# Turning a third of the softmax tiles with VectorE and transfers instead of TensorE, and other first transfers, in a fused attention and gated feed-forward kernel

## The chip, the core and the metric

One of the eight cores of a Trainium2 chip. The metric is device time of one execution in microseconds (us). Before the change: 924.59 us, median of three runs from 923.99 to 927.79.

## What is computed

Attention whose weights below the row's maximum less tau are set to zero, then a feed-forward network with a convolution of three taps over the tokens and a gate. Sizes: 8 batches, 8 heads, 576 tokens, 64 columns per head; 512 model columns, 1024 inner columns.

```python
scores = scale * np.matmul(q, k.transpose(0, 1, 3, 2))
thresh = np.max(scores, axis=-1, keepdims=True) - tau
scores = np.where(scores >= thresh, scores, -1000000000.0)
attn = np.exp(scores - np.max(scores, axis=-1, keepdims=True))
attn = attn / (np.sum(attn, axis=-1, keepdims=True) + 1e-09)
attn_out = np.matmul(attn, v)
...
h = np.maximum(x @ w_in, 0.0)
for k in range(K):
    conv_out += conv_w[k][None, None, :] * hp[:, k:k + S, :]
gate = 1.0 / (1.0 + np.exp(-conv_out))
return (h * gate @ w_out).astype(np.float32)
```

## The kernel before, in words

Two heads form a pair; a batch has four pairs. The 576 tokens of a batch are five tiles, four of 128 and one of 64, in two chunks: tiles 0 and 1, then tiles 2, 3 and 4. A *unit* is one tile of one pair; 20 units make a batch, 160 the kernel.

**A unit** (`unit`, from L516). TensorE writes the scores of each head to PSUM (`ps_s`, L537 in batch 0 and for the small tile, L544 elsewhere). VectorE takes the row maximum (`top`, L552), one of three engines makes the threshold (`limit`, L556 or L558), ScalarE the exponential (`exp`, L561), and VectorE sets what lies below the threshold to zero and sums the row (`mask`, L564). A small chain forms the inverse of the sum (L581 to L588), and `norm` (L595 on ScalarE, L597 elsewhere) scales the tile `em`, 128 rows by 2 x 576 columns.

**Transposes** (from L608). The product with v needs `em` turned. TensorE turns it in nine blocks of 128 x 128 (L626), in two groups of four into a bank of PSUM (`ps_t`), and the ninth blocks of a pair's tiles together in a last group. ScalarE evicts each group to `eT` (L621), 512 columns at a time, or the ninth blocks side by side. `attend` (L676, L685) multiplies `eT` by v for two pairs at once; ScalarE and VectorE split the result into a high and a low part, `x` (L692, L695).

**Feed-forward.** `mm1` (L713) multiplies `x` by the first weights; `relu` (L728), three taps (`tap0` L732 or L734, then L748), tanh (L757) and the gate (L755) follow, and a split into `gh` and `gl`. `mm2` (L786) multiplies by the second weights; ScalarE evicts 128 tokens to `ot` (L793) and SP's queue writes them out (L794).

**Loads.** SP's queue issues the loads of k (L451, L487), q (L452, L502), v (L513) and of the weights (L363), and copies inside SBUF, `halves` (L477), that bring heads from one half of the partitions to the other for `ks`, `q1` and `q2`. At the start, ScalarE's queue issues the loads of the first pair's k and of the first three pieces of weights.

**The order.** Nothing runs where it is written. Each operation goes to a `Plan` (L83) with its engine, a cost in ns, what it reads and writes, and a due time: the number of its unit less a lead from the table `AHEAD`. `Plan.run` plays all engines forward and takes, on each, the ready operation with the earliest due time; it keeps buffers and costs of its own. An operation with several possible engines can leave its first one when that has more than `BACKLOG` ns of work; `NORM`, `TAP` and `LOW` name the first engine of normalizations, first taps and low parts; `KEEP` and `SWITCH` order TensorE's kinds of matmul; `MOE` says how `mm1` and `mm2` alternate. What comes out is a fixed list of instructions for each engine. Four `em`, two `eT`, two `q1`, two `q2` and two `v` buffers exist.

Of the kernel before, what the change touches and what calls it, by code (L numbers as in the profile page):

```python
# [20 lines left out]
AHEAD = {'s': 6.25, 's4': 7.75, 't': 3.5, 'a': 3.5, 'prep': 4.25, 'w': 2.5, 'load': 7.75}  # L21
# [13 lines left out]
BACKLOG = {'pool': 6860.0, 'dve': 120.0, 'act': 9000000000.0}  # L35
WRATE = (1.225, 1.745)
ALT = 11.76
# [4 lines left out]
EARLY = 1  # L42
# [6 lines left out]

JOINT = 2  # L50

KEEP = {'rows': 2.304, 'cols': 1.613, 'turn': 3.226, 'full': 2.304}
# [30 lines left out]
class Plan:  # L83
# [32 lines left out]
    def run(self):  # L116
# [35 lines left out]
        while events:  # L152
# [25 lines left out]
            for e in ready:  # L178
# [4 lines left out]
                while ready[e]:  # L183
# [6 lines left out]
                    if e == home or load[home] + max(free[home] - t, 0.0) > BACKLOG[home]:  # L190
# [55 lines left out]
def tile_tau_attention_gated_ffn(  # L246
# [14 lines left out]
    nc = tc.nc  # L261
# [32 lines left out]

    def const(name, shape, dtype):
        return plan.buf(cpool, name, 1, shape, dtype, name)
# [30 lines left out]
    def sp(n):  # L327
        return 2.6 * n
# [13 lines left out]
    def split(src, n, name, high, low, hr, lr, queue="sp"):  # L342
# [17 lines left out]
        w = AHEAD["w"]  # L360

        def load():
            (nc.sync if queue == "sp" else nc.scalar).dma_start(flat().bitcast(I64), src)  # L363
# [16 lines left out]
        if queue == "sp":  # L380
            op("sp", sp(2 * n), load, w=[hi, lo], ahead=w + AHEAD["load"])
        else:
            op("act", 450, load, w=[hi, lo], ahead=90, late=sp(2 * n) + LATENCY["sp"])
# [37 lines left out]
    def load_weight(i):  # L421
        if i < W1N:
            src, dst, c, f = w_in, w1, i % NCB, i // NCB
        else:
# [4 lines left out]
            src[c * P:(c + 1) * P, f], WN, f"stage_{i}", h, l, *((x, (c, f.start)) for x in dst), "act" if i < 3 else "sp"  # L429
# [14 lines left out]
    def prep_rows(i, b, p, o, w, tag):  # L444
# [3 lines left out]
        a = AHEAD["prep"]  # L448

        if i:  # L450
            op("sp", sp(S + D), lambda: nc.sync.dma_start(k[:], kp[b, p]), w=[(k, 0), (k, 1)], ahead=a + 2)  # L451
            op("sp", sp(2 * w), lambda: nc.sync.dma_start(q[:], qd[b, p, :, :, o:o + w]), w=[(q, 0), (q, 1)], ahead=a + 2)  # L452
        else:
            for j, on in enumerate((slice(0, CH), slice(CH, S + D))):
                op(
                    "act", 450, lambda on=on: nc.scalar.dma_start(k[:, on], kp[b, p, :, on]), w=[(k, j)], ahead=210 - 10 * j,
                    late=1500 + sp(CH) * (1 + j)
                )
                op(
                    "sp", sp(w) + 400, lambda j=j: nc.sync.dma_start(q[:, j], qd[b, p, :, j, o:o + w]), w=[(q, j)], ahead=210 - 10 * j  # L460
                )
# [21 lines left out]
    def prep_k(b, p, ks):  # L483

        a = AHEAD["prep"]
# [11 lines left out]
    def prep_q(i, b, p, q1, q2):  # L497
# [3 lines left out]
        a = AHEAD["prep"]  # L501
# [9 lines left out]
    def load_v(i, b, p):  # L511
        vt = plan.buf(wk, "v", 2, [P, NBLK, D], F32, f"v_{i}")
        op("sp", sp(NBLK * D), lambda: nc.sync.dma_start(vt[:], vc[b, p]), w=[(vt, 0)], ahead=AHEAD["prep"])  # L513
        return vt

    def unit(u, k, q1, q2, o, n):  # L516
# [8 lines left out]
        a = AHEAD["s" if 2 * n > P else "s4"]  # L525
# [81 lines left out]

    def transposes(u, ems, tiles, eT):  # L608


        em, n, off = ems[-1]

        def group(i, reads, parts, *evacs, width=4 * P):
# [3 lines left out]
                "pe", width * 0.852, lambda: parts(pt), w=[(pt, 0)], r=reads + [(ident, 0)], ahead=AHEAD["t"], kind="turn"  # L617
            )
            for k, (w, dst, src) in enumerate(evacs):
                op(  # L620
                    "act", act(w, True), lambda dst=dst, src=src: nc.scalar.activation(dst(), src(pt), AF.Copy),  # L621
                    w=[(eT, (off, i, k))], r=[(pt, 0)], ahead=AHEAD["t"]
# [15 lines left out]
        if n < P:  # L638
# [9 lines left out]
        full, small = ([x for x in ems if (x[1] < P) == y] for y in (False, True))  # L648
# [3 lines left out]
        def odd(pt):  # L652
            for x in full + small:
                turn(pt, x[2], x[0], 8 if x[1] == P else 3.5)

        parts = [(w, lambda: eT[:, 8, :w], lambda pt: pt[:, :w])]
        for _, m, at in small:
            for j in range(2):
                parts.append((
                    m, lambda j=j: eT[j * D:(j + 1) * D, 4, at:at + m], lambda pt, j=j: pt[D:, w + j * m:w + (j + 1) * m]  # L660
# [3 lines left out]
    def attend(of, w, parts):  # L664

        pas = [plan.buf(ps_t, "ps_t", 2, [P, 512], F32, f"pa_{i}") for i, *_ in of]
        a = AHEAD["a"]
# [287 lines left out]
```

## Time and profile before

| | before |
|---|---|
| median of three runs | 924.59 us |
| the profiled execution | 925.54 us |
| its span, first to last instruction | 923.8 us |
| granted clock of TensorE | 0.996 |
| packets of the transfers | 77,926, of them 18,560 under 512 bytes |
| bytes moved | 104.02 MB |
| HBM read and written | 58.88 and 9.44 MB |

PE is TensorE's matmul, PEld its weight load, DVE VectorE, ACT ScalarE, POOL GpSimd; SP's and ACT's queues issue transfers (SPq, ACTq). A group's row reads: line, engine, operation, what is written and read, shape, count, then busy us and mean ns of one, then the idle time just before and what ended it. A timeline's row: start and length in us, engine, line, operation and count.

### The profile page before, as it was taken

How to read it: one execution, taken by the hardware profiler on the slowest of the kernel's cores; microseconds unless marked ns; L12 is line 12 of the kernel's file. 1: busy time of each engine (PE TensorE's matmuls, PEld its weight loads, DVE VectorE, ACT ScalarE, POOL GpSimd, SP SyncE). 2: the span in 40 equal slices, each digit the busy share in tenths (PEclk: the TensorE clock that was granted, in tenths of full speed). 3: DMA queues.
4: the chain of work that ended last, by engine and by line, in shares of the span. 5: the costliest groups of instructions: out<-in, count | busy, mean ns of one | idle time of the engine just before them, and what ended most of it. 6: DMA issues, size and time to landing. Idle time of an engine off the chain costs nothing.

```text
span 923.8 us, 19667 instructions
## 1 busy us (share of the span) xinstructions
PE 896.7 (97%) x6308; PEld 731.8 (79%) x6308; DVE 741.1 (80%) x1853; ACT 701.2 (76%) x1590; POOL 582.1 (63%) x1028
## 2 busy tenths in 40 slices
PE   5989899999999999999999999999999999999998
PEld 2446588878889788879888787887888888887897
DVE  5988999979868798878967789886977879896643
ACT  5888898878678787869768687786958788785653
POOL 3665887767747586666746677675865757664422
PEclk9999999999999999999999999999999999999999
DMA  6643363355341652345423453416523265221000
GB/s 211 200 151 128 97 166 101 111 146 167 87 122 40 176 150 83 84 115 140 122 91 81 133 148 103 120 59 166 161 85 95 55 175 140 83 79 60 13 24 34
DMA packets 77926, 104.02 MB, mean 113 GB/s; under 512 B 18560, under 2 KB 49536, under 8 KB 77824
## 3 DMA queue, kind: packets, MB, share of 16 engines
q1 hardware_dynamic: 76960, 100.86, 38.6%
q10 hardware_dynamic: 864, 1.90, 0.6%
q8 instruction: 51, 0.84, 0.4%
q14 instruction: 51, 0.42, 0.1%
HBM read 58.88 MB, written 9.44 MB: 74 GB/s over the span
## 4 chain that ended last, share of the span: by engine, by line
PE 79%; ACT 9%; DVE 6%; issue 2%; DMA 2%; POOL 1%; SPq 0%; ACTq 0%; POOLq 0%; DVEq 0%
PE po L786 21%; PE ph L713 16%; PE ps_t L626 13%; PE pa L685 12%; PE ps_s L544 11%; PE ps_s L537 4%; ACT eT L621 2%; PE pa L676 2%; DVE em L564 2%; ACT em L561 2%; DVE few L552 1%; DVE t L748 1%; PE pw_stage L394 1%; DMA q<-in_qd_dram 1%; ACT hp L728 1%
## 5 line engine op out<-in xcount | busy, mean ns | idle before, releaser
L597 POOL TENSOR_SCALAR em<-em,few 128x576 f32<-128x576 f32 x285 | 258.3, 914 | 36.9 <-DVE few L588 27.3
L564 DVE SCALAR_TENSOR_TENSOR em<-ps_s,few,em 128x576 f32<-128x576 f32 x288 | 228.1, 812 | 51.0 <-ACT em L561 44.9
L713 PE MATMUL ph<-x,w1h 128*128 128x322 f32 (+1 forms) x1024 | 243.2, 305 | 0.7 <-ACT hp L728 0.7
L552 DVE TENSOR_REDUCE few<-ps_s 128x1 f32<-128x576 f32 x288 | 210.8, 748 | 29.4 <-PE ps_s L537 15.2
L561 ACT ACTIVATE em<-ps_s,few 128x576 f32<-128x576 f32 x288 | 206.7, 743 | 30.9 <-DVE few L552 26.0
L621 ACT ACTIVATE eT<-ps_t 128x512 f32<-128x512 f32 (+2 forms) x416 | 203.3, 512 | 16.9 <-PE ps_t L626 15.2
L626 PE MATMUL ps_t<-ident,em 128*128 128x128 f32 x1312 | 187.7, 276 | 4.6 <-DVE x L695 1.7
L626 PEld LDWEIGHTS ps_t<-ident,em 128*128 128x128 f32 x1312 | 152.3, 141 | 34.2 <-POOL em L597 11.0
L713 PEld LDWEIGHTS ph<-x,w1h 128*128 128x128 f32 x1024 | 174.9, 189 | 3.7 <-issue 1.8
L748 DVE SCALAR_TENSOR_TENSOR t<-hp,cw,t 128x255 f32<-128x255 f32 (+1 forms) x256 | 151.9, 597 | 25.9 <-ACT t L732 18.8
L544 PE MATMUL ps_s<-ks,q 128*128 128x288 f32 x896 | 155.0, 304 | 2.6 <-DVE em L564 1.6
L713 PE MATMUL ph<-x,w1l 128*128 128x322 f32 (+1 forms) x512 | 151.1, 295 | 0.0
L544 PEld LDWEIGHTS ps_s<-ks,q 128*128 128x128 f32 x896 | 129.0, 188 | 13.8 <-issue 4.6
L324 POOL TENSOR_TENSOR gl<-t,gh 128x255 fp32r<-128x255 f32 (+9 forms) x192 | 121.4, 644 | 29.4 <-ACT gh L765 29.2
L685 PE MATMUL pa<-eT,v 128*64 128x320 f32 (+1 forms) x1024 | 133.3, 412 | 0.0
L685 PEld LDWEIGHTS pa<-eT,v 128*64 128x64 f32 x1024 | 70.9, 138 | 59.9 <-issue 16.7
L786 PE MATMUL po<-w2h,gh 128*128 128x512 f32 x288 | 118.1, 410 | 0.0
L786 PE MATMUL po<-w2h,gl 128*128 128x512 f32 x288 | 113.0, 392 | 0.5 <-POOL gl L324 0.5
L786 PE MATMUL po<-w2l,gh 128*128 128x512 f32 x288 | 113.1, 393 | 0.0
L713 PEld LDWEIGHTS ph<-x,w1l 128*128 128x128 f32 x512 | 96.6, 189 | 0.1
L755 DVE SCALAR_TENSOR_TENSOR t<-t,hp 128x321 f32<-128x321 f32 (+1 forms) x128 | 70.8, 554 | 14.3 <-ACT t L757 13.6
L757 ACT ACTIVATE t<-t 128x321 f32<-128x321 f32 (+1 forms) x128 | 56.9, 445 | 24.4 <-DVE t L748 24.1
(69 smaller groups left out, 1019.6 us busy)
## 6 DMA issues: line engine op xcount, KB each, us to landing
q<-q SPq DMA_DIRECT2D x336, 64.0 KB, 2.0
v<-in_vc_dram SPq DMA_DIRECT2D x64, 288.0 KB, 3.3
k<-in_kp_dram SPq DMA_DIRECT2D x35, 320.0 KB, 3.6
out_dram<-ot SPq DMA_DIRECT2D x36, 256.0 KB, 2.0
xk<-in_kt_dram SPq DMA_DIRECT2D x28, 288.0 KB, 3.3
ks<-xk SPq DMA_DIRECT2D x56, 144.0 KB, 2.4
xq<-in_qt_dram SPq DMA_DIRECT2D x56, 128.0 KB, 2.3
stage<-in_w_out_dram SPq DMA_DIRECT2D x8, 512.0 KB, 3.5
```

Of the source, the lines that this page charges most:

```text
L324: engines[e].tensor_tensor(dst, x, y, op=ALU.subtract)
L544: nc.tensor.matmul(ps[:, c, :CH], lhsT=q[:, h, o:o + n], rhs=k[:, h, c * CH:(c + 1) * CH], start=(i == 0), stop=(i == 1))
L552: nc.vector.tensor_reduce(few[:rows, nm], ps[:rows, :, :CH], op=ALU.max, axis=mybir.AxisListType.XY, negate=True)
L561: nc.scalar.activation(view(), ps[:rows, :, :CH], AF.Exp, bias=few[:rows, nm])
L564: nc.vector.scalar_tensor_tensor(view(), ps[:rows, :, :CH], few[:rows, th], view(), op0=ALU.is_ge, op1=ALU.mult, accum_out=few[:rows, total])
L597: engines[e].tensor_scalar(sl, sl, by, to, op0=ALU.mult, op1=ALU.add)
L621: "act", act(w, True), lambda dst=dst, src=src: nc.scalar.activation(dst(), src(pt), AF.Copy),
L626: nc.tensor.transpose(out=pt[:, at:at + P], in_=em[:, int(b * P):int(b * P) + P], identity=ident[:])
L685: nc.tensor.matmul(pa[j * D:(j + 1) * D, :w], lhsT=vt[:, blk, :], rhs=eT[:, blk, :w], start=False, stop=(r == 3))
L713: nc.tensor.matmul(ph[:, :an], lhsT=w1[w][:, cb, fs], rhs=xs[cb][:, h, :an], start=(cb == 0 and i == 0), stop=(cb == NCB - 1 and i == 2))
L748: nc.vector.scalar_tensor_tensor(t[:, :kn], hp[:, k:kn + k], cw[:, 3 * f + k:3 * f + k + 1], t[:, :kn], op0=ALU.mult, op1=ALU.add)
L786: nc.tensor.matmul(po[:], lhsT=x[:, f, at:at + P], rhs=w[:, f, :], start=(f == 0 and i == 0), stop=(f == NFB - 1 and i == 2))
```

## The change

**Squares.** In batches 1 to 7, five of the sixteen full tiles of a batch (units 5, 9, 12, 15 and 18 of its 20) are not turned by TensorE. VectorE turns the whole normalized `em` in place, each square of 32 x 32 by itself, in one instruction over 1152 columns. Then 16 transfers on SP's queue bring the squares to their places in `eT`: each takes 32 partitions and nine pieces of 32 columns (128 bytes). These tiles also leave the group of the ninth blocks; where the remaining ones are not side by side, ScalarE evicts them one by one.

**First transfers.** The first pair's k comes in two halves, one from each queue, in between its q; the first three pieces of weights move from ScalarE's queue to SP's, behind them.

**Last output.** The last 128 tokens are evicted and written in two halves, by ScalarE and VectorE, from both queues.

**Tables.** Leads have values of their own for the first 24 units (`AHEAD0`, `BACKLOG0`); normalizations start from ScalarE and GpSimd in turn; a first tap can be VectorE's; the other numbers of the planner change too.

```diff
-AHEAD = {'s': 6.25, 's4': 7.75, 't': 3.5, 'a': 3.5, 'prep': 4.25, 'w': 2.5, 'load': 7.75}
+AHEAD = {'s': 6.25, 's4': 8.25, 't': 3.5, 'v': 5.25, 'a': 2.25, 'prep': 5.0, 'w': 0.75, 'load': 10.0}
+AHEAD0 = {'s': 6.5, 's4': 9.25, 't': 3.0, 'v': 3.5, 'a': 3.5, 'prep': 2.0, 'w': 2.25, 'load': 7.0}
+HEAD = 24
...
-NORM = (('pool',), ('pool',))
-NEAR = 8
+NORM = (('dve',), ('act', 'pool'))
+NEAR = 0
 PIECES = 12
-TAP = ('act', 'pool', 'act', 'act')
-LOW = ('pool', 'pool')
+TAP = ('pool', 'act', 'dve', 'pool', 'act', 'act')
+LOW = ('pool',)
...
-MOE = (2, 2)
+MOE = (4, 2)
...
+SQUARES = (0, 0, 0, 0, 0, 1, 0, 0, 0, 1, 1, 0, 1, 0, 0, 1, 1, 0, 1, 0)
+SQFROM = 24
...
     def sp(n):
-        return 2.6 * n
+        return SPW * n + 150
...
+    def squares(u, n):
+        return n == P and u >= SQFROM and SQUARES[u % len(SQUARES)]
...
-        if n < P:
+        if squares(u, n):
+            a = lead("v")
+            op("dve", dve(2 * S), lambda: nc.vector.transpose(em[:], em[:]), w=[(em, 0), (em, 1)], ahead=a, port=True)
+            for x in range(4):
+                for y in range(4):
+                    def move(x=x, y=y):
+                        nc.sync.dma_start(
+                            eT[y * 32:(y + 1) * 32, :, off + x * 32:off + (x + 1) * 32],
+                            em[x * 32:(x + 1) * 32, :].rearrange("p (k y i) -> p y k i", y=4, i=32)[:, y]
+                        )
+
+                    op("sp", 480, move, w=[(eT, (off, x, y))], r=[(em, 0), (em, 1)], ahead=a)
+        elif n < P:
...
+        full = [x for x in ems if x[1] == P and not squares(x[3], P)]
+        small = [x for x in ems if x[1] < P]
...
+            op("act", 450, lambda: load_k(nc.scalar, first), w=[(k, 0)], ahead=210, late=LATENCY["sp"] + 700)
+            op("sp", 700, lambda: load_q(0), w=[(q, 0)], ahead=210, late=700)
+            op("sp", 800, lambda: load_k(nc.sync, second), w=[(k, 1)], ahead=209, late=500)
+            op("sp", 600, lambda: load_q(1), w=[(q, 1)], ahead=208, late=500)
...
+        x, y = slice(0, DO // 2), slice(DO // 2, DO)
+        op("act", act(DO // 2, True), lambda: nc.scalar.activation(ot[:, x], po[:, x], AF.Copy), w=[(ot, 0)], r=[(po, 0)])
+        op("dve", dve(DO // 2), lambda: nc.vector.tensor_copy(ot[:, y], po[:, y]), w=[(ot, 1)], r=[(po, 0)])
+        op("act", 450, lambda: nc.scalar.dma_start(rows[:, x], ot[:, x]), r=[(ot, 0)], late=LATENCY["sp"])
+        op("sp", sp(DO // 2), lambda: nc.sync.dma_start(rows[:, y], ot[:, y]), r=[(ot, 1)])
```

Counted over the whole list of instructions, TensorE has 315 transposes fewer (997 instead of 1312). ScalarE has 160 normalizations instead of 3, 186 evictions of 512 columns instead of 256 into one `eT`, 11 of 256 columns instead of 64 and 71 of 128, and 69 first taps instead of 96. GpSimd has 128 normalizations instead of 285, 158 thresholds instead of 71 and 58 first taps instead of 32. VectorE has 35 square turns, 102 thresholds instead of 183 and one first tap. SP issues 1256 transfers instead of 692.

The order on SP in the second half of batch 1, before: the loads of v (L513) for two pairs, then the copies of k's heads (`ks`, L477) for batch 2.

```order
L452 DMA q_2526<-in_qd_dram 128x2x64
L513 DMA v_2529<-in_vc_dram 128x576
L513 DMA v_2555<-in_vc_dram 128x576
L477 DMA ks_0_2531<-ks_0_2531 64x576
L477 DMA ks_0_2531<-xk_0_2482 64x576
L477 DMA ks_1_2575<-ks_1_2575 64x576
```

The same place after; L660 are the moves, L526 and L490 the v loads and the copies.

```order
L461 DMA q_2550<-in_qd_dram 128x2x64
L526 DMA v_2553<-in_vc_dram 128x576
L526 DMA v_2571<-in_vc_dram 128x576
L660 DMA eT_2561<-em_2441 32x9x32 x16
L490 DMA ks_0_2541<-ks_0_2541 64x576
L490 DMA ks_0_2541<-xk_0_2492 64x576
L660 DMA eT_2646<-em_2615 32x9x32 x3
L490 DMA ks_0_2541<-xk_0_2492 64x576
L660 DMA eT_2646<-em_2615 32x9x32 x13
L834 DMA out_dram<-ot_2638 128x512
```

Between the v loads and the copies of the next batch's k now stand the 32 moves of two tiles.

On VectorE, after, near the same place: L565 is the maximum, L577 the mask, L594 and L601 the inverse, L786 the later taps.

```order
L565 TENSOR_REDUCE few_2569<-ps_s_1_2563 128x1
L577 SCALAR_TENSOR_TENSOR em_2615,few_2569<-ps_s_0_2556,few_2569,em_2615 128x576
L577 SCALAR_TENSOR_TENSOR em_2615,few_2569<-ps_s_1_2563,few_2569,em_2615 128x576
L594 TENSOR_SCALAR few_2569<-few_2569 128x2
L601 RECIPROCAL few_2569<-few_2569 128x2
L565 TENSOR_REDUCE few_2657<-ps_s_0_2641 128x1
L565 TENSOR_REDUCE few_2657<-ps_s_1_2651 128x1
L656 STREAM_TRANSPOSE em_2615<-em_2615 128x1152
L786 SCALAR_TENSOR_TENSOR t_0_2691<-hp_0_2321,cw,t_0_2691 128x255
```

Before, such a tile left VectorE with its inverse; now VectorE has it a second time, after the normalization elsewhere and two maxima of the next tile.

At the start of SP's list, before:

```order
L460 DMA q_0_79<-in_qd_dram 128x256 x2
L451 DMA k_96<-in_kp_dram 128x640
L363 DMA stage_107<-in_w_in_dram 128x512
L452 DMA q_1_124<-in_qd_dram 128x2x256
L513 DMA v_130<-in_vc_dram 128x576
```

And after:

```order
L468 DMA q_0_79<-in_qd_dram 128x256
L465 DMA k_77<-in_kp_dram 128x352
L468 DMA q_0_79<-in_qd_dram 128x256
L375 DMA stage_97<-in_w_in_dram 128x512
L375 DMA stage_107<-in_w_in_dram 128x512
L375 DMA stage_119<-in_w_in_dram 128x512
L375 DMA stage_131<-in_w_in_dram 128x512
L460 DMA k_151<-in_kp_dram 128x640
L461 DMA q_1_161<-in_qd_dram 128x2x256
```

The second half of the first k and three pieces of weights have come over from ScalarE's queue, and the second pair's k (`k_151`, before `k_96`) stands behind four pieces of weights where it stood ahead of them.

More of the change, by code (lines that the diff above doesn't have):

```diff
@@ L340, in pool1, with split @@
         return n * 0.9 + 225
-    def split(src, n, name, high, low, hr, lr, queue="sp"):
+    def split(src, n, name, high, low, hr, lr):
         stage = plan.buf(wk, "ks", 4, [P, 2, S], U32, name)
@@ L378, in f4 @@
             nc.vector.scalar_tensor_tensor(v(U32), words()[0], 29, v(U32), op0=ALU.logical_shift_right, op1=ALU.bitwise_or)
[L380 to L383, printed above, removed]
+        op("sp", sp(2 * n), load, w=[hi, lo], ahead=w + lead("load"))
         op("act", act(n), f0, w=[a], r=[hi], ahead=w)
@@ L616, in group @@
             op(
-                "pe", width * 0.852, lambda: parts(pt), w=[(pt, 0)], r=reads + [(ident, 0)], ahead=AHEAD["t"], kind="turn"
+                "pe", width * 0.852, lambda: parts(pt), w=[(pt, 0)], r=reads + [(ident, 0)], ahead=lead("t"), kind="turn"
             )
```

80 lines of the change are left out of this document (46 added, 34 removed).

## The prediction

> **What bounds the kernel now.** I read the page's busy times first, then the shares of the chain that ended last, then the table of stretches, cut where the softmax of batch 1 begins (125.3 us) and where that of batch 7 ends (860.4 us).
>
> ```profile
> PE 896.7 (97%) x6308; PEld 731.8 (79%) x6308; DVE 741.1 (80%) x1853; ACT 701.2 (76%) x1590; POOL 582.1 (63%) x1028
> PE 79%; ACT 9%; DVE 6%; issue 2%; DMA 2%; POOL 1%; SPq 0%; ACTq 0%; POOLq 0%; DVEq 0%
> 0.00:125.30 125.30, 105.97 (x641) 65.33 (x643) 106.23 (x253) 99.09 (x207) 76.74 (x128) 0.97 0.50 156
> 125.30:860.40 735.10, 730.97 (x5304) 614.80 (x5305) 608.66 (x1551) 570.07 (x1302) 484.36 (x857) 1.00 0.41 113
> 125.30:213.30 88.00, 87.53 (x637) 72.53 (x638) 78.81 (x207) 71.85 (x160) 62.19 (x109) 1.00 0.48 135
> ```
>
> The columns of a stretch are its length, then the busy time of PE, PEld, DVE, ACT and POOL, the clock and the DMA engines' share. In the 735.1 us of batches 1 to 7 PE idles for 4.1 us; DVE has 126 us of air, ACT 165 us. In the 88 us of the last row DVE is 90% busy and PE still idles for only 0.5 us, so a neighbour at 90% does not cost PE anything here. Batch 0 is another matter: PE idles for 19.3 of 125.3 us. So PE work taken away from batches 1 to 7 shortens the kernel until another resource is full. One that the busy times leave out is SP's queue, which issues the transfers one after another; it comes below.
>
> **PE.** 35 tiles (five in each of seven batches) lose nine transposes each: 315 of the 1312. The groups give the pipelined length of one; the time it holds PE is read from the starts in the timeline.
>
> ```profile
> L626 PE MATMUL ps_t<-ident,em 128*128 128x128 f32 x1312 | 187.7, 276 | 4.6 <-DVE x L695 1.7 <-ACT eT L621 1.5 <-POOL em L597 1.3
> 417.55 1.04 PE L626 MATMUL ps_t<-ident,em 128*128 128x128 f32 x8
> 418.34 0.48 PE L786 MATMUL po<-w2h,gh 128*128 128x512 f32 x1
> ```
>
> Eight hold it from 417.55 to 418.34, 0.79 us, so 99 ns each. By the group's busy time it would be 143 ns, but that counts the overlap with the next matmul. 315 x 0.099 = 31.2 us less (45 us by the other reading, which is the far end). The work between 125.3 and 860.4 us then fits in 735 - 31 = 704 us.
>
> **ACT, DVE and POOL must fit in those 704 us.**
>
> ```profile
> L621 ACT ACTIVATE eT<-ps_t 128x512 f32<-128x512 f32 x288 | 166.2, 602 | 14.2 <-PE ps_t L626 13.3
> L621 ACT ACTIVATE eT<-ps_t 128x256 f32<-128x256 f32 x64 | 25.5, 398 | 1.9 <-PE ps_t L626 1.9
> L595 ACT ACTIVATE em<-em,few x3: 852/867/922, 88.4 to 102.8; 128x576 f32<-128x576 f32 x3
> L732 ACT ACTIVATE t<-hp,cw 128x255 f32<-128x255 f32 x48 | 24.7, 514 | 4.1 <-POOL hp L723 2.3 <-POOL gl L324 1.0
> L597 POOL TENSOR_SCALAR em<-em,few 128x576 f32<-128x576 f32 x285 | 258.3, 914 | 36.9 <-DVE few L588 27.3 <-DVE few L558 6.1 <-PE ps_s L544 1.1
> L552 DVE TENSOR_REDUCE few<-ps_s 128x1 f32<-128x576 f32 x288 | 210.8, 748 | 29.4 <-PE ps_s L537 15.2 <-PE ps_s L544 12.2
> L558 DVE TENSOR_SCALAR few<-few,ntau 128x1 f32<-128x1 f32 x183 | 34.7, 207 | 1.0
> L558 POOL TENSOR_SCALAR few<-few,ntau 128x1 f32<-128x1 f32 x71 | 26.9, 379 | 37.0 <-DVE few L552 25.9 <-DVE few L588 9.0 <-DMA v<-in_vc_dram 0.3
> ```
>
> ACT takes 160 normalizations where it had 3: 157 x 0.867 = 136 us, seven eighths of it (119) in batches 1 to 7. It loses 70 evictions of 512 columns (42 us), 27 first taps (27 x 0.514 = 14 us), and the ninth-block evictions change from 64 of 256 columns to 11, with 71 of 128 (about even). 570 + 119 - 42 - 14 = 633 us, 90% of 704.
>
> DVE's squares are not in the trace: 1152 columns at 1.3 ns each, the reduction's 748 ns for 576, make 1.5 us; the same at one square pass without PSUM could be 1.1. I take 1.3: 35 x 1.3 = 46 us. It gives 81 of the thresholds to POOL (81 x 0.207 = 17, of which 15 here). 609 + 46 - 15 = 640 us, 91%. The page "VectorE: DVE Perf Modes" of the Trainium skill, section The three transpose paths, gives 311 ns for one 128x128 turn in 32x32 blocks (16-bit data); by an estimate from it nine blocks take 2.8 us, DVE would be 692 us busy, 98%, and the forecast would stand on a thinner edge. No trace here shows it.
>
> POOL loses 157 x 0.914 = 143 us of normalizations (126 here), gains 87 thresholds of 0.379 us and 26 taps: about 400 us, 57%. By the 88 us row, ACT and DVE at 90% cost PE little.
>
> **SP's queue.** 560 issues are added to it, 16 per tile, in order with the loads of k, q and v and the copies that fill ks and q1, q2. First what it does in batches 1 to 7, then how closely issues follow each other.
>
> ```profile
> q<-q SPq DMA_DIRECT2D x324, 64.0 KB, 2.0
> v<-in_vc_dram SPq DMA_DIRECT2D x55, 288.0 KB, 3.3
> k<-in_kp_dram SPq DMA_DIRECT2D x28, 320.0 KB, 3.6
> out_dram<-ot SPq DMA_DIRECT2D x31, 256.0 KB, 2.2
> ks<-xk SPq DMA_DIRECT2D x51, 144.0 KB, 2.4
> xk<-in_kt_dram SPq DMA_DIRECT2D x25, 288.0 KB, 3.3
> xq<-in_qt_dram SPq DMA_DIRECT2D x52, 128.0 KB, 2.3
> ks<-ks SPq DMA_DIRECT2D x25, 144.0 KB, 2.6
> q<-in_qd_dram SPq DMA_DIRECT2D x26, 64.0 KB, 3.2
> 329.08 2.46 SPq L477 DMA_DIRECT2D q<-q  x4
> 331.59 0.88 SPq L502 DMA_DIRECT2D xq<-in_qt_dram  x1
> 332.57 0.38 SPq L451 DMA_DIRECT2D k<-in_kp_dram  x1
> L477 SPq DMA_DIRECT2D q<-q x336: 461/541/1837, 98.1 to 834.4; - x168
> L452 SPq DMA_DIRECT2D q<-in_qd_dram x35: 551/597/1341, 5.1 to 814.2; - x35
> L513 SPq DMA_DIRECT2D v<-in_vc_dram x64: 327/376/1396, 5.8 to 849.2; - x64
> ```
>
> Four copies of 64 partitions take from 329.08 to 331.59, 0.63 us each back to back; alone one takes 0.46, 0.51 with the 0.05 us to the next. 400 copies (324 + 51 + 25) at 0.63 are 252 us; the other 217 at about 0.53 (0.38 to 0.58 and the gap) are 115. That is 367 of 735 us now. A move has 32 partitions of nine pieces of 128 bytes; no row shows one. If it is like a lone copy, 0.51: 560 x 0.51 = 286, 653 in all. If like a copy in a row, 0.63: 353, 720 in all, over the 704. A second dimension could add what the q load of two pieces has over the v load, 0.551 - 0.327 = 0.22: 0.73 each, 409, 776 in all. I take the middle of the two copies, 0.57, because a move names half the partitions of a copy and follows others like it: 319, so 686 us, 97% of 704. SP then nearly ties with PE, and what stands behind 16 moves (9 us) comes late: k, q1 and q2 for the scores, and v. A wait at the head holds all of it, and attend waits for the last of its moves. I charge 1% of the 704 us as new PE idle time, 8 us (between 0 and 30, the end where the gain is gone).
>
> **The DMA engines.** 560 x 32 x 9 = 161,280 packets of 128 bytes, 20.6 MB, come to those of the page.
>
> ```profile
> q1 hardware_dynamic: 76960, 100.86, 38.6%
> DMA packets 1007, 1.05 MB, mean 174 GB/s; under 512 B 610, under 2 KB 610, under 8 KB 1007
> q1 hardware_dynamic: 1007, 1.05, 62.4%
> DMA packets 770, 1.23 MB, mean 246 GB/s; under 512 B 105, under 2 KB 361, under 8 KB 770
> q1 hardware_dynamic: 770, 1.23, 88.6%
> ```
>
> The last four lines are 412 to 418 us and 340 to 345 us: 59.9 us of engine time for 610 small and 397 large packets, 70.9 us for 105 and 665. Solved for both, a small packet takes 32 ns. 161,280 x 32 ns / 16 = 323 us, over 704 us and beside 0.41 x 735 = 301: 89% at most. At the bytes' share it would be 8% more. The engines hold. On "DMA: Bandwidth & Descriptors" the Trainium skill (Specifications) asks for pieces of at least 512 bytes, as smaller ones are read, changed and written back, which speaks against moves of 128; its section Why small descriptors are slow (HBM only) exempts SBUF to SBUF. The fit sides with the second; by the first the last rival below would decide.
>
> **The two ends.** In batch 0 the first weights go behind the first scores' q and k on SP; they were on ACT's queue and read first at 10.27 us.
>
> ```profile
> 4.56 1.33 PE L537 MATMUL ps_s<-k,q 64*128 64x288 f32 x4 [4.56 <-ACT q L466]
> 10.27 0.65 ACT L366 ACTIVATE stage_f<-stage 128x512 f32<-128x512 f32 x1
> 920.29 0.60 ACT L793 ACTIVATE ot<-po 128x512 f32<-128x512 f32 x1 [4.89 <-PE po L786]
> ```
>
> The first matmul waits for k and q until 4.56 us, and the splitting of weights, which could fill PE's 19.3 idle us, starts late. I take a fifth, 4 us (from -4, pair 1's k now later, to 10). At the end ACT and DVE each evict half of the last 512 columns (0.60 becomes about 0.4): 0.3 us. The new orders of MOE, TAP and the AHEAD numbers move work that PE has to do anyway; I cost them at nothing beyond this, covered by PE's queue.
>
> **Sum.** The profiled execution took 925.5 us, 1.7 outside its span and 0.95 above the median of 924.6. 925.5 - 31.2 + 8 - 4 - 0.3 = 898, less the 0.95: 897 us.
>
> **Rivals.** *SP becomes the bound* (slower). If a move costs 0.73, batches 1 to 7 take 776 us instead of 735: 924.6 + 41 - 4.3 = 961 us. The gain is gone from (735 - 367) / 560 = 0.66 us per move, and from 0.68 the kernel is slower by more than half a percent. For it: copies in a row already take 0.63. Against: SP is half idle now, and copies in a row name 64 partitions. Chance 0.26; with waits in a full queue it can reach 975.
>
> *The moves give back what PE gains* (same). At 0.66 to 0.67 SP needs 737 to 742 us, 924.6 + 2 (or 7) - 4.3 = 922 to 927 us; a tie that costs PE all 30 us ends there too. Chance 0.11.
>
> *PE's time is freer than I read*. A transpose is worth 143 ns and nothing ties: 924.6 - 45 - 4.3 = 875 us. Against: the starts 0.79 us apart. Chance 0.05.
>
> *The DMA engines fill* (slower). If a piece of 128 bytes costs the mean packet's time, 0.386 x 923.8 x 16 / 76,960 = 74 ns, 746 us are added to 301: over 1040 us in those batches and over 1200 in all. The small packets' 32 ns speak against it. Chance 0.02. It is the first of the two rules of the skill named above that would make it.
>
> **Chances.** Half a percent, 4.6 us, is about the least change that a measurement of this kernel can tell from none. The forecast keeps 0.56, and with the freer PE faster is 0.61, same 0.11, slower 0.28. The range runs from 876 to 970, so that it holds the forecast, the tie and the SP case at 0.73; its own range is 880 to 915.
>
> **What would show it.** Right: PE's busy time near 865 us, over 95% of its span from batch 1 on, the moves 0.51 to 0.6 us apart, SP waiting now and then. Wrong: moves more than 0.66 apart and SP never waiting; PE idle before scores or attend, released by a q, ks or eT transfer; DVE squares of over 2 us; DMA share near 1.

## The result, and the profile after

| | before | after |
|---|---|---|
| median (runs) | 924.29 us (4) | 1017.64 us (4) |
| lowest to highest | 923.76 to 927.79 | 1016.59 to 1019.56 |
| profiled execution, span | 925.54, 923.8 us | 1017.31, 1015.5 us |
| granted clock of TensorE | 0.996 | 0.973 |

Before counts one run more here than ahead of the prediction.

The changed kernel takes 1.1003 times as long, 95% interval 1.0972 to 1.1035: 93 us more, where some 28 us less was forecast. 1017.6 us lies beyond the range (876 to 970), and beyond the 975 us allowed to the rival in which SP becomes the bound. The busy times of after, the shares of the chain that ended last, and the stretch from unit 20's inverse of the sum (the start of batch 1's softmax results) to unit 159's, which was 735.1 us before:

```profile
PE 915.1 (90%) x5993; PEld 717.7 (71%) x5993; DVE 767.2 (76%) x1809; ACT 763.1 (75%) x1662; POOL 482.1 (47%) x984
PE 39%; ACT 15%; DMA 14%; DVE 12%; SPq 11%; issue 5%; POOL 3%; DVEq 0%; ACTq 0%; POOLq 0%
```

```profile
119.97:949.71 829.74, 754.87 (x5062) 610.68 (x5061) 637.35 (x1516) 628.25 (x1376) 397.62 (x820) 0.97 0.51 125
```

No engine is full. In batches 1 to 7 PE is busy for 755 of 830 us, where it was busy for 731 of 735. The chain, 79% PE before, now passes through ACT, transfers, DVE and SP's queue in turn. A chain through everything suggests something that all of them wait for in common. The timeline of SP's queue shows a candidate, over 60 us (rows in between left out at the dots):

```profile
499.78 0.55 SPq L490 DMA_DIRECT2D ks<-xk  x1
500.43 3.10 SPq L490 DMA_DIRECT2D q<-q  x5
503.58 0.58 SPq L515 DMA_DIRECT2D xq<-in_qt_dram  x1
504.26 0.40 SPq L460 DMA_DIRECT2D k<-in_kp_dram  x1
504.70 1.75 SPq L490 DMA_DIRECT2D q<-q  x3
506.50 0.58 SPq L515 DMA_DIRECT2D xq<-in_qt_dram  x1
507.13 0.91 SPq L526 DMA_DIRECT2D v<-in_vc_dram  x2
508.13 11.68 SPq L660 DMA_DIRECT2D eT<-em  x16
...
532.88 10.53 SPq L660 DMA_DIRECT2D eT<-em  x16
543.45 1.25 SPq L490 DMA_DIRECT2D q<-q  x2
544.74 0.58 SPq L515 DMA_DIRECT2D xq<-in_qt_dram  x1
546.62 11.35 SPq L660 DMA_DIRECT2D eT<-em  x16
558.08 2.46 SPq L490 DMA_DIRECT2D q<-q  x4
```

```profile
L660 SPq DMA_DIRECT2D eT<-em x560: 586/612/1623, 146.7 to 957.4; - x187
```

Nearly each row ends 0.04 to 0.12 us before the next one starts; the one break of note in the 60 us is of 1.3 us, ahead of 546.62. Sixteen moves of a tile (L660) take 10.5 to 11.7 us, 0.66 to 0.73 each. In the last row, the line's own, the three numbers are the shortest, middle and longest issue in ns. Added up from 120 to 955 us, 835 us: 1175 issues, 702 us (556 moves 359, the 619 others 342), 69 us in gaps under 0.3 us between them, and 65 us in longer gaps, the real waits. Before, the longer gaps were 356 of the 730 us from 130 to 860. SP's queue is full but for the waits at its head.

How a full queue reaches the others is seen at those who wait for what it carries. Waits of ACT in batches 1 to 7 of before:

```profile
ACT q L463 <- DMA q<-in_qd_dram: 9.5, 8, 1.8
ACT xk L488 <- DMA xk<-in_kt_dram: 1.9, 3, 0.7
```

and of after, first ACT, then PE, then SP's queue itself (us in all, times, longest):

```profile
ACT q L476 <- DMA q<-in_qd_dram: 35.3, 14, 5.9
ACT xk L501 <- DMA xk<-in_kt_dram: 24.7, 10, 5.6
```

```profile
PE ps_t L642 <- DVE x L733: 21.4, 10, 5.1
PE ps_t L642 <- ACT eT L637: 17.2, 11, 4.4
PE ps_s L557 <- DMA q<-q: 10.9, 12, 2.1
PE ps_s L557 <- DMA ks<-xk: 10.9, 6, 2.5
PE pa L714 <- DMA eT<-em: 5.4, 8, 1.3
```

```profile
SPq L490 <- ACT q L516: 11.6, 9, 4.4
```

A load of q or k can stand behind 16 moves. ACT waits for it up to 5.9 us, 60 us in all where it was 11, and what ACT has queued behind (evictions, exponentials) is late with it. The copy that needs ACT's result then stands at the head of SP's queue, as in the last row, and holds the moves behind. PE itself waits little for the moves (5.4 us): it waits mostly for those who are late (DVE's x, ACT's eT). That is why counting only PE's direct waits on transfers (27 us) understates the queue.

### The profile page after: what moved, and what is told of

It is laid out like the page before. It is cut to its first block, busy times and chain, and to the rows that moved or that the text cites. A ratio compares the mean times of both kernels' runs of the same rounds, so it can differ in the third digit from the quotient of the medians.

```text
span 1015.5 us, 19906 instructions
## 1 busy us (share of the span) xinstructions
PE 915.1 (90%) x5993; PEld 717.7 (71%) x5993; DVE 767.2 (76%) x1809; ACT 763.1 (75%) x1662; POOL 482.1 (47%) x984
## 4 chain that ended last, share of the span: by engine, by line
PE 39%; ACT 15%; DMA 14%; DVE 12%; SPq 11%; issue 5%; POOL 3%; DVEq 0%; ACTq 0%; POOLq 0%
PE po L824 10%; PE ph L751 9%; PE ps_s L557 6%; SPq L660 6%; PE pa L723 5%; PE ps_t L642 5%; SPq L490 4%; DMA q<-q 4%; DVE em L577 4%; DVE few L565 3%; ACT em L574 3%; DMA xk<-in_kt_dram 3%; ACT em L608 3%; ACT eT L637 3%; DMA q<-in_qd_dram 2%
## 5 line engine op out<-in xcount | busy, mean ns | idle before, releaser
L577 DVE SCALAR_TENSOR_TENSOR em<-ps_s,few,em 128x576 f32<-128x576 f32 x288 | 228.7, 812 | 56.7 <-ACT em L574 48.4
L565 DVE TENSOR_REDUCE few<-ps_s 128x1 f32<-128x576 f32 x288 | 211.3, 749 | 30.5 <-PE ps_s L557 22.2
L642 PE MATMUL ps_t<-ident,em 128*128 128x128 f32 x997 | 156.6, 286 | 46.0 <-DVE x L733 21.6
L557 PE MATMUL ps_s<-ks,q 128*128 128x288 f32 x896 | 158.3, 307 | 25.2 <-DMA q<-q 10.9
L642 PEld LDWEIGHTS ps_t<-ident,em 128*128 128x128 f32 x997 | 119.7, 145 | 80.5 <-issue 30.8
L637 ACT ACTIVATE eT<-ps_t 128x512 f32<-128x512 f32 (+3 forms) x364 | 161.1, 469 | 17.1 <-PE ps_t L642 15.8
L786 DVE SCALAR_TENSOR_TENSOR t<-hp,cw,t 128x255 f32<-128x255 f32 (+1 forms) x256 | 148.7, 588 | 30.2 <-POOL t L772 24.5
L336 POOL TENSOR_TENSOR gl<-t,gh 128x255 fp32r<-128x255 f32 (+9 forms) x192 | 117.7, 625 | 71.1 <-ACT gh L803 67.4
L608 ACT ACTIVATE em<-em,few 128x576 f32<-128x576 f32 x160 | 138.0, 866 | 10.7 <-DVE few L601 9.7
L723 PE MATMUL pa<-eT,v 128*64 128x320 f32 (+1 forms) x1024 | 138.3, 422 | 0.0
L610 POOL TENSOR_SCALAR em<-em,few 128x576 f32<-128x576 f32 x128 | 117.9, 921 | 25.8 <-DVE few L601 16.6
L733 DVE TENSOR_TENSOR x<-pa,x 128x256 fp32r<-128x256 f32 (+1 forms) x64 | 28.9, 452 | 79.6 <-ACT x L730 79.4
```

Source lines behind the costliest of these rows:

```text
L557: nc.tensor.matmul(ps[:, c, :CH], lhsT=q[:, h, o:o + n], rhs=k[:, h, c * CH:(c + 1) * CH], start=(i == 0), stop=(i == 1))
L565: nc.vector.tensor_reduce(few[:rows, nm], ps[:rows, :, :CH], op=ALU.max, axis=mybir.AxisListType.XY, negate=True)
L577: nc.vector.scalar_tensor_tensor(view(), ps[:rows, :, :CH], few[:rows, th], view(), op0=ALU.is_ge, op1=ALU.mult, accum_out=few[:rows, total])
L608: nc.scalar.activation(sl, sl, AF.Identity, scale=by, bias=to)
L610: engines[e].tensor_scalar(sl, sl, by, to, op0=ALU.mult, op1=ALU.add)
L642: nc.tensor.transpose(out=pt[:, at:at + P], in_=em[:, int(b * P):int(b * P) + P], identity=ident[:])
```

## The experiments

No version with squares beat the kernel before. Medians in us; each ratio is to the kernel before, run on the same chip. "Batches" is the stretch from unit 20's inverse to unit 159's, the column before it where the first of the two lies; both are read from one profiled execution each.

| run | median | ratio, 95% interval | unit 20 | batches |
|---|---|---|---|---|
| before | 924.29 | 1 | 125.3 | 735.1 |
| ends alone | 929.72 | 1.0050, 1.0031 to 1.0069 | 127.7 | 736.4 |
| new code, old tables, no squares | 939.24 | 1.0143, 1.0101 to 1.0185 | 132.7 | 740.7 |
| new tables, no squares | 945.82 | 1.0200, 1.0175 to 1.0226 | 120.6 | 758.8 |
| after (five squares) | 1017.64 | 1.1003, 1.0972 to 1.1035 | 120.0 | 829.7 |
| five squares, old tables | 1033.4 | 1.1132, 1.1074 to 1.1191 | 135.1 | 839.2 |
| two squares, new tables | 964.49 | 1.0400, 1.0372 to 1.0427 | 120.0 | 783.1 |
| two squares, old tables | 942.58 | 1.0180, 1.0153 to 1.0207 | 134.2 | 747.8 |
| two squares, old tables, later attend | 940.94 | 1.0156, 1.0117 to 1.0194 | 137.2 | 744.1 |
| before + 560 unread loads | 1009.37 | 1.0864, 1.0816 to 1.0912 | 125.7 | 821.2 |
| before + 224 unread loads | 927.83 | 1.0023, 1.0006 to 1.0041 | 122.4 | 735.9 |
| before + 224 unread moves | 936.94 | 1.0125, 1.0100 to 1.0150 | 125.3 | 746.7 |
| new tables + 224 unread loads | 971.41 | 1.0497, 1.0459 to 1.0534 | 119.8 | 789.3 |

### Is it the squares or the tables?

The first run takes away the squares, the second the tables:

```diff
-SQFROM = 24
+SQFROM = 100000
```

> The changed kernel without the squares: all tiles are turned by TensorE again, every other table and transfer of the change stays. Theory (SP's queue is full): SP's issues fall from 1256 to 696, about 370 us of the 735 of batches 1 to 7, TensorE is the bound again and the time is 915 to 930 us. Rival (the new tables and orders cost the time): it stays above 980 us.

```diff
-AHEAD = {'s': 6.25, 's4': 8.25, 't': 3.5, 'v': 5.25, 'a': 2.25, 'prep': 5.0, 'w': 0.75, 'load': 10.0}
+AHEAD = {'s': 6.25, 's4': 7.75, 't': 3.5, 'v': 5.25, 'a': 3.5, 'prep': 4.25, 'w': 2.5, 'load': 7.75}
-NORM = (('dve',), ('act', 'pool'))
+NORM = (('pool',), ('pool',))
...
```

> The changed kernel with the squares, the first transfers and the last output, but with the leads, backlogs, first engines and other numbers of the kernel before (the lead of the squares stays 5.25). Theory (SP's queue): about as slow as the changed kernel, 990 to 1040 us. Rival (the tables cost the time): 890 to 930 us.

Without squares 945.8 us, which neither side said: the squares carry some 72 of the 93 us, and what else has changed, which the forecast costed at nothing, carries the rest. With squares and the old tables 1033.4 us, as the theory said: the new tables are not what makes it slow with squares, they make the full queue somewhat less bad. The page and the same stretch of the first run:

```profile
PE 911.1 (97%) x6308; PEld 731.2 (78%) x6308; DVE 739.2 (78%) x1817; ACT 801.1 (85%) x1745; POOL 476.2 (51%) x942
```

```profile
120.60:879.36 758.76, 748.87 (x5328) 618.71 (x5327) 607.32 (x1521) 662.35 (x1449) 391.70 (x777) 1.00 0.40 110
```

PE is busy for 749 of 759 us at the full clock: PE bounds again, but the stretch takes 24 us more than before; over the whole kernel PE is busy for 911 us with the same 6308 matmuls that took 897 before.

### Is it the queue?

Nothing of the change, but 16 unread loads on SP for each tile that the change squares; every transpose stays on TensorE:

```diff
+        if n == P and u >= 24 and SQUARES[u % 20]:
+            for j in range(16):
+                op("sp", 480, lambda j=j: nc.sync.dma_start(idle[:, j % 4], qd[u // 20, 0, :, :, j * 16:(j + 1) * 16]),
+                    w=[(idle, j % 4)], r=[(em, 0), (em, 1)], ahead=5.25)
```

> The kernel before, with all transposes on TensorE, and 16 more issues on SP per tile that the change turns with squares: loads of 128 x 2 x 16 from HBM into a place that nothing reads, so that no engine waits for them; the planner may place them once the tile is normalized. Their form of issue takes about as long as a move (0.65 us). Theory (the rate of issue on SP): SP's own need is 367 + 560 x 0.70 = 759 us in batches 1 to 7 against 735, and waits in the full queue add to it: 950 to 1020 us. Rival (the way of a tile is longer: square, moves, landing, buffers held): nothing waits for these loads, so 920 to 935 us.

1009.4 us, in the theory's range. Nobody reads these loads, they write 512 bytes per partition over and over, and the kernel loses 83 us to the before of its chip. Its busy times, chain and the first waits of PE:

```profile
PE 928.3 (92%) x6308; PEld 748.6 (74%) x6308; DVE 751.7 (75%) x1808; ACT 713.1 (71%) x1619; POOL 590.6 (59%) x1044
PE 41%; SPq 16%; DMA 12%; ACT 10%; DVE 9%; POOL 6%; issue 6%; ACTq 0%; POOLq 0%; DVEq 0%
```

```profile
PE ps_t L635 <- ACT eT L630: 20.2, 12, 5.2
PE ps_t L635 <- DVE x L704: 18.3, 11, 3.0
```

They look like those of after: PE at 92%, the chain through SP's queue, and the same two waits of the transposes at the top. In batches 1 to 7 the issues and their short gaps take 759 us of SP's queue, and 62 us of longer waits stay, 821 us together. The issues alone, with the tables of before, bring most of the loss.

With 224 of them (two tiles a batch, `SQUARES` with ones at units 9 and 15 only), the queue has room:

> The kernel before with 16 loads that nothing reads at two tiles a batch (units 9 and 15), 224 in all. SP needs 367 + 157 = 524 of 735 us, so it is not full on average. Theory in its first form (only a full queue costs): 924 to 932 us. Second form (bursts of 10 us delay the copies behind them): 935 to 950 us. Rival (only the tile's longer way costs): 924 to 928 us.

927.8 us, 0.2% above before. So, with the tables of before, 224 issues cost some 2 us and 560 cost 83: it is not one price per issue, but what happens when SP has little air left. Where between the two the loss begins was not tried.

### Another queue

Two squares on SP (the first two lines of the edit), then the moves of two and of five squares on GpSimd's queue (the other lines):

```diff
-SQUARES = (0, 0, 0, 0, 0, 1, 0, 0, 0, 1, 1, 0, 1, 0, 0, 1, 1, 0, 1, 0)
+SQUARES = (0, 0, 0, 0, 0, 0, 0, 0, 0, 1, 0, 0, 0, 0, 0, 1, 0, 0, 0, 0)
...
-                        nc.sync.dma_start(
+                        nc.gpsimd.dma_start(
...
-                    op("sp", 480, move, w=[(eT, (off, x, y))], r=[(em, 0), (em, 1)], ahead=a)
+                    op("pool", 1000, move, w=[(eT, (off, x, y))], r=[(em, 0), (em, 1)], ahead=a, late=2000)
```

> The changed kernel with two squares a batch (units 9 and 15) instead of five. Theory (SP's queue): SP needs 367 + 224 x 0.70 = 524 us, it is no longer full, and 126 transposes less give 12 us: 900 to 915 us, below the kernel without squares by about 12. Rival (each square costs, by its longer way): a share of two fifths of the loss, 950 to 965 us.

> Two squares a batch as in the run before, with their 16 moves issued from GpSimd's queue instead of SP's (costed at 1 us each for the planner). GpSimd has room for 224 us. Theory (the moves stand in the way of q, k and v on SP): SP is as without squares, the 126 transposes less come through as 12 us, 930 to 942 us, against 946 without squares and 964 with SP's moves. Rival (the tile's way is longer, em and eT are held): it stays at 958 to 970 us, whoever issues.

> The changed kernel with all moves on GpSimd's queue. What an issue costs there no trace shows. Theory (a queue's rate of issue is what is paid): SP is freed, and GpSimd's 401 us of work in batches 1 to 7 plus 560 issues decide: at 0.3 us each 569 us, TensorE is the bound again and 915 to 930 us come out; at 1 us each 961 us, GpSimd is the bound and the kernel takes over 1150 us. Rival (the way of a tile): near 1018 us as with SP.

Two squares on SP 964.5 us (the theory's 900 to 915 missed, the rival's 950 to 965 hit); on GpSimd 991.4 us (ratio 1.0712, 1.0688 to 1.0737), slower than either side said; five on GpSimd 1140.7 us (1.2329, 1.2292 to 1.2365; two runs), which again neither side said. GpSimd's timeline with five, then the line's own row and the sum of GpSimd's waits for squares (us in all, times, longest):

```profile
499.97 3.62 POOL L660 DMA_DIRECT2D eT<-em  x6
504.17 1.81 POOL L660 DMA_DIRECT2D eT<-em  x3 [0.59 <-DMA eT<-em]
506.02 0.83 POOL L610 TENSOR_SCALAR em<-em,few 128x576 f32<-128x576 f32 x1
506.82 1.42 POOL L336 TENSOR_TENSOR xk<-xk,ks 128x576 fp32r<-128x576 f32 x1
508.21 0.73 POOL L336 TENSOR_TENSOR q<-xq,q 128x256 fp32r<-128x256 f32 x1
514.52 6.07 POOL L660 DMA_DIRECT2D eT<-em  x10 [5.59 <-DVE em L656]
```

```profile
L660 POOL DMA_DIRECT2D eT<-em x560: 609/609/852, 148.6 to 1083.1; - x187
POOL eT L660 <- DVE em L656: 31.4, 9, 5.6
```

An issue is no cheaper there (0.61 us), and it stands in one line with GpSimd's own arithmetic, which others wait for. At 508.94 GpSimd stops for 5.59 us, because the next move in its order needs a square that VectorE has not made. GpSimd is not full (busy for 751 us, 66% of the span), so these two runs are no test of the rate of issue: they show what waits in the order of an engine cost that has other work. The queue was moved from an engine that computes nothing to one that does.

### Why two squares cost although the queue has room

One run has two squares and the old tables; the next has besides 1.25 units more between squares and attend (the edit is of the second against the first):

```diff
-AHEAD = {'s': 6.25, 's4': 7.75, 't': 3.5, 'v': 5.25, 'a': 3.5, 'prep': 4.25, 'w': 2.5, 'load': 7.75}
-AHEAD0 = AHEAD
+AHEAD = {'s': 6.25, 's4': 7.75, 't': 3.5, 'v': 5.25, 'a': 2.25, 'prep': 4.25, 'w': 2.5, 'load': 7.75}
+AHEAD0 = dict(AHEAD, a=3.5)
```

> Two squared tiles a batch (units 9 and 15) with the tables of the kernel before, so that of the change only the tiles' way, the ends and the plan's price of a transfer's issue stay (the price at 2.6 ns a column as before). With the new tables the two tiles cost 964.5 against 945.8 without them, 18.7 us. Theory 1, the way itself: the tiles' moves share one in-order queue with the loads and shifts that scores wait for, and each holds the other up whatever the tables: the same 15 to 20 us over the kernel before, 938 to 948 us. Theory 2, the tables: the new short leads (attend 2.25 units instead of 3.5) leave the moves no time, and with the old leads two tiles cost nothing or pay their 12.6 us of transposes: 912 to 928 us.

> Two squared tiles with the tables before (942.6 us), but the attends planned 2.25 units ahead of their place instead of 3.5, so that a squared tile has 3 units (about 16 us) instead of 1.75 (9 us) for its square, 16 moves and landing, which take some 14 us together. Theory 1 (the attends, and the transposes and scores queued behind them, wait for moves that have no time): 915 to 932 us. Theory 2 (it is not the time but what the moves and the scores' shifts do to each other on the queue): 938 to 950 us.

942.6 and 940.9 us. The intervals of the two overlap, so the later attend shows no gain clear of noise: the 9 us of slack were not the main cause. But 942.6 must be held against 939.2 us for the same program without squares, not against before. In the batches, 747.8 less 740.7 is 7.1 us net; with 126 transposes (12.5 us at the prediction's 99 ns) saved, the tiles' way costs some 20 us by this estimate.

Moves alone, read by nobody, all transposes kept, in place of the unread loads:

```diff
+                        nc.sync.dma_start(
+                            idle[y * 32:(y + 1) * 32, x],
+                            em[x * 32:(x + 1) * 32, :].rearrange("p (k y i) -> p y k i", y=4, i=32)[:, y, :, :IW]
+                        )
```

> The kernel before with the moves of two tiles a batch, issued at the same places from the same tiles, but into a scratch tile that nobody reads (pieces of 12 instead of 128 bytes, since the memory has room for no more), and with all transposes kept on TensorE and no square on VectorE. Theory 1 (two squares cost because those who need the moved tile wait for it): the moves alone cost as little as the loads did, 924 to 930 us. Theory 2 (the moves themselves, 288 small pieces each on the same memory and queue, slow the rest): 936 to 945 us.

936.9 us: the batches take 746.7 us, 11.6 us more than before and 10.8 more than with as many unread loads (9 by the ratios in the table, as the profiled execution of the loads, 922.91 us, is their fastest). Yet SP's issues from 130 to 860 us add up to the same (473 against 475 us), and so do the transfers' shares in the batches, first of the loads, then of the moves:

```profile
q1 hardware_dynamic: 127440, 85.46, 45.7%
```

```profile
q1 hardware_dynamic: 134608, 82.57, 44.5%
```

So some 9 to 11 of the 20 us come with the moves themselves, by something that neither SP's time nor the engines' share shows. The waits tell where it comes out: ACT waits for its loads of q and k for 23.0 us, with the unread loads for 9.2, and PE idles for 10.0 us instead of 2.8. Why those loads are later stays open, and the planned order of the two runs is not quite the same. The pieces were 12 bytes here, not 128, so the figure is no exact price for the real moves.

The same loads under the new tables:

> The new tables, no tile squared (all transposes on TensorE), and for the two tiles a batch 16 unread loads each on SyncE, as in the run of 224 unread loads that cost the kernel before 2 us (927.83 against 925). To be held against 945.8 us (new tables, no loads) and 964.5 us (two tiles squared). Theory 1 (it is the waits between moves and the shifts that others need, not the issues): 944 to 952 us. Theory 2 (the new tables leave SyncE's queue no slack, so 16 issues in a row make scores late): 957 to 967 us.

971.4 us, slower than either side said, where the old tables took them for 2 us: in the batches +30.5 against +0.9 us. PE now waits for the copies, for which the same view without the loads has no row:

```profile
PE ps_s L558 <- DVE em L578: 9.3, 15, 2.2
PE ps_t L643 <- ACT eT L638: 7.0, 8, 1.4
PE ps_s L558 <- DMA q<-q: 6.6, 7, 2.5
```

That is no less than two squares cost there net of the transposes they save (24.4 us in the batches): under the new tables SP's issues have a price long before the queue is full. Which number makes it was not tried.

### Where the tables' 20 us lie

Four runs without squares put one group of tables back each; a fifth (new code, old tables) put all back; a sixth took before and only the new ends; a last one nudged one lead of before (`'t': 3.5` to `3.25`).

```diff
 e11: AHEAD and AHEAD0 of before
 e12: NORM of before
 e13: NORM, NEAR, TAP, LOW, MOE, BACKLOG of before
 e14: WRATE, ALT, EARLY, KEEP and the price of a transfer of before
```

> The new tables without squares (945.8 us), but with the leads of the kernel before (score, attend, prep, weight and load leads); the choice of engines, the rates and the prices stay new. The tables cost 20 us together. Theory 1 (the leads cost them): 924 to 933 us. Theory 2 (the engines cost them: half of the normalisations on ScalarE, which is 85% busy then): 939 to 949 us.

> The new tables without squares (945.8 us), but with the normalisation of every tile on GpSimd as before (that is, none on ScalarE); the rest stays new. Theory 1 (the leads cost the 20 us): 938 to 950 us. Theory 2 (ScalarE's 160 normalisations of 0.87 us cost them): 924 to 935 us.

> The new tables without squares (945.8 us), but every choice of engine as before (normalisation, taps, low halves, gate, backlogs); leads, rates and prices stay new. Theory 1 (the engine choices cost the 20 us together, ScalarE being 85% busy where it was 76%): 925 to 934 us. Theory 2 (the tables are only right together, and any mix is as slow): 940 to 952 us.

> The new tables without squares (945.8 us), but the rates of the weights and outputs, the times for which TensorE keeps to one kind of matmul and the price of a transfer as before; leads and engine choices stay new. Theory 1 (the engine choices cost the 20 us): 940 to 952 us. Rival (TensorE's order, set by the rates and keeping times, costs it): 926 to 934 us.

943.5, 948.1, 944.2 and 949.4 us, or 1.0201, 1.0254, 1.0208 and 1.0255 times the before of their chips, against 1.0200 with all tables new: no group alone brings anything back. ScalarE's 160 normalizations, the suspect with ScalarE at 85%, are not it by themselves.

> The kernel before with the first transfers and the last output of the change alone; no squares, all tables as before. By the prediction's terms 4.3 us less: 920 to 922 us. Rival (the weights' loads now hold up the second pair's k on SP): 925 to 930 us.

> The changed program with all tables of the kernel before and no tile squared: what stays of the change is its first transfers, its split last output and its code. Theory 1 (the tables cost the 20 us, only all of them together bring it back): 926 to 934 us, as the run with the ends alone (929.7). Rival (the code around them costs): 940 to 950 us.

> The kernel before with one number changed: transposes planned 3.25 units ahead instead of 3.5. No work is added or taken. Theory 1 (the order before is fitted so closely that a nudge costs): 932 to 945 us. Rival (orders nearby are as good): 922 to 929 us.

Ends alone 929.7 us, 4.6 more than before where the prediction's terms said 4.3 less; new code with old tables 939.2, between the two sides; the nudge 926.4 (ratio 1.0006, 0.9988 to 1.0024). So before is no needle's point: this nearby order is as good. And putting all tables back leaves the program 13 us above its before (1.0143). The ends give some 5 of these, and the program itself some 9. Without squares it plans one thing differently: the ninth blocks. Evictions to `eT` of before:

```profile
L621 ACT ACTIVATE eT<-ps_t 128x256 f32<-128x256 f32 x64 | 25.5, 398 | 1.9 <-PE ps_t L626 1.9
```

and of the new program with old tables:

```profile
L637 ACT ACTIVATE eT<-ps_t 128x128 f32<-128x128 f32 x64 | 15.3, 301 | 0.1
L637 ACT ACTIVATE eT<-ps_t 128x256 f32<-128x256 f32 x32 | 12.5, 390 | 1.3 <-PE ps_t L642 1.3
```

The new code compares the tiles' places in the order in which they come, finds half of the groups not side by side, and evicts them one by one, although no square was taken out. That is 2.3 us more of ScalarE, and another order from batch 0 on. I take this for the cause of the 9 us, since the diff shows no other; it was not tried by itself, so it is not shown.

The table of runs then splits the 94.6 us of batches 1 to 7: ends 1.3, code 4.3, tables 18.1, squares 70.9. The ends' 1.3 is no more than the nudge's 1.4. The split holds in this order of adding only: on top of five squares the new tables win 9.5 us (839.2 to 829.7) instead of losing 18.1. In batch 0 the ends lose 2.4 and the code 5.0 us, and the new tables win 12.1, which is why they seem to cost only 7 us in the whole. Which numbers of the tables make the 18 us stays open.

## Why the prediction was wrong, point by point

- **The step that failed: SP's price.** "I take the middle of the two copies, 0.57 ... so 686 us, 97% of 704". An issue of a move takes 0.646 us and the next starts 0.05 us later: 0.69, nearer to the upper bound of 0.73 that the row with the second dimension gave. The 619 others cost 342 us plus 43 in gaps, 0.62 each, by which the prediction's 617 come to 384 (367 there). With 560 x 0.69, 388 us, SP needs 772 us, over the 735 it had. By the prediction's own threshold (0.66) this alone is the rival's case. The argument "a move names half the partitions of a copy" was wrong: 288 pieces cost more than a copy of 64 partitions.
- **The rival was right in kind and too small.** It set the batches equal to SP's need, 776 us, and the need was 772. They took 830, because 65 us of waits at the queue's head stayed: a queue in order that feeds chains (load, ACT, copy, scores) was not filled to the last us in any run here. With the unread loads, which have neither the new tables nor the new code, 62 us stayed.
- **"The new orders ... I cost them at nothing ... covered by PE's queue": wrong.** The tables cost 18 us in batches 1 to 7 without any square, and the code 4. PE is the bound there, and its queue did not cover them: it idles for 9.9 us instead of 4.1 and is busy for 18 us more (749 and 731), at a clock of 1.00 in both.
- **The 8 us of friction**, new idle time of PE, stood for a near tie. Behind the full queue PE idled for 75 us of the batches, 71 more than before, and five squares cost 70.9 us there, after their saving in transposes.
- **The transposes did leave PE** (997 in place of 1312), but the forecast of 865 us busy failed: 915. Busy time is not work, as the 911 us without squares for the matmuls of before show. In batches 1 to 7 PE is busy for 755 us where 731 less the 31 of the transposes would be 700. Part of these 55 us is the clock. After is at half clock in eleven stretches of batches 1 to 7, of 3.4 or 6.8 us, 48 us in all, which takes up to 24 us; each comes with a wait of PE, or waits close together, of 1.6 us or more, and before has none there. One of them, from the row of an attend that waited for moves:

```profile
474.55 0.72 PE L714 MATMUL pa<-eT,v 64*64 64x320 f32 x2 [1.29 <-DMA eT<-em]
474.80:480.50 5.70, 5.34 (x24) 2.29 (x24) 2.84 (x7) 1.97 (x7) 3.73 (x5) 0.70 0.69 174
```

The second row is a stretch, with a clock of 0.70. Not every wait of this length brings one.
- **Engines: right.** Forecast in 704 us: ACT 633, DVE 640, POOL about 400. Measured in the batches: 628, 637, 398. Squares and normalizations:

```profile
L656 DVE STREAM_TRANSPOSE em<-em 128x1152 f32<-128x1152 f32 x35 | 48.1, 1374 | 5.5 <-POOL em L610 3.5 <-POOL hp L763 1.8 <-ACT em L608 0.2
L608 ACT ACTIVATE em<-em,few 128x576 f32<-128x576 f32 x160 | 138.0, 866 | 10.7 <-DVE few L601 9.7 <-issue 0.3
```

The square takes 1.37 us (1.3 taken). The estimate from the Trainium skill's page "VectorE: DVE Perf Modes", The three transpose paths, was 2.8 us; the trace halves it.

- **Transfers: right that they hold.** The share in batches 1 to 7, from 125 to 860 us before and from 120 to 955 us after, with the moves' row:

```profile
q1 hardware_dynamic: 66512, 81.78, 40.2%
```

```profile
q1 hardware_dynamic: 235423, 102.84, 50.8%
eT<-em SPq DMA_DIRECT2D x556, 36.0 KB, 1.9
```

(0.508 x 835 - 0.402 x 735) x 16 = 2059 us for 235,423 - 66,512 = 168,911 more packets, of which 556 x 288 = 160,128 are the moves' pieces: 12 to 13 ns each, under half of the 32 taken. By the rule of the Trainium skill's page "DMA: Bandwidth & Descriptors" (Specifications) that pieces under 512 bytes are read, changed and written back they should have been dear; the trace sides with that page's other section, Why small descriptors are slow (HBM only), which exempts transfers from SBUF to SBUF.

- **The head came as sized, for another reason.** The first matmul starts at 3.85 us (4.56 before) and unit 20 at 120.0 (125.3), 5.3 us earlier with 4 forecast. But with the ends alone unit 20 is 2.4 us later, and with the new tables on top of ends and code 12.1 us earlier: the tables bring it, not the first transfers.

Of what was named as showing it wrong, moves over 0.66 apart, SP hardly waiting (65 of 835 us), and PE idle before scores and attend by q, ks and eT transfers came true; squares over 2 us (1.37) and a DMA share near 1 (0.51) did not.

## What to carry to other kernels

Before work goes from a full engine to transfers, count the issues of the queue, with the gap after each and the dearest neighbouring row as price, and stay well under full: loads that nobody read cost 2 us at 224 and 83 us at 560, and under other tables 224 of them cost some 26. A queue in order is a resource like an engine, and when it is full, those who wait are less the readers of the new transfers than all whose loads stand behind. Tables that reorder work, or move it between engines that have room, are not free where one engine is the bound, and a run of the new program with the new feature off shows how much of the loss is not the feature's.

## What the runs showed of the hardware

- An issue on SP's queue takes 0.65 us for a move of 32 partitions x 9 pieces in after (0.66 with two squares, where the queue has room), 0.63 for an unread load (the mean of the run with 224), and 0.58 for a copy of 64 partitions (325 from 120 to 955 us of after, 189 us; 0.54 before). On GpSimd's queue a move takes 0.61 us.
- A move of 288 small pieces lands 1.9 us after its issue, as fast as a copy of 64 partitions (2.0), also when the queue is full.
- The granted clock was lower where TensorE was busy for less: 0.996 before and 1.000 without squares (97% busy), 0.973 after (90%), 0.916 in the run of 1140.7 us (84%). In after it fell to half for 3.4 or 6.8 us at a time, at waits of TensorE.
